# Second product of a split-word Winograd FFN: two matmuls for three, one of them 512 columns wide

## The chip, the core and the metric

The kernel runs on one NeuronCore of a Trainium2 chip. The metric is device time in microseconds (us). The kernel before takes 871.11 us, the median of three runs (870.78, 871.11 and 873.4). A profile of one execution shows its span, from the first to the last instruction, as 867.2 us. In this document PE is TensorE, PEld its weight loads, ACT is ScalarE, DVE is VectorE, POOL is GpSimd and SP is SyncE, which issues most DMAs.

## The reference

A linear attention with a normalisation feeds a feed-forward layer:

```python
kv  = einsum('bhsd,bhse->bhde', k, v)          # 8 batches, 8 heads, 576 tokens, 64 dims
o   = einsum('bhsd,bhde->bhse', q, kv)
x   = o / sqrt(mean(o*o) + 1e-6) * g_norm      # -> x: 4608 tokens x 512
h   = x @ w_in                                  # 512 -> 2048
g   = h * tanh(softplus(h))                     # Mish
out = g @ w_out                                 # 2048 -> 512, float32
```

The change touches the last line alone: `g @ w_out`, called the second product here.

## The kernel before

**Words.** Matrix operands are kept as two fp32r words each, a high one (the value rounded to fp32r) and a low one (what is left). A product of two such operands is made of three fp32r matmuls: low times high, high times low, high times high. `split` (L121) makes the words: ACT casts to the high word (L122), DVE subtracts to get the low word (L123).

**Blocks.** Each of the two big products is cut into 2 x 2 blocks and done with seven block products in place of eight (Winograd's form). The list `PROD` names them: A11*B11, S1*T1, A22*T4, S2*T2, A12*B21, S4*B22, S3*T3. The S forms are sums and differences of blocks of the left matrix, the T forms of the right one. The function `group` (L494) holds the order: its steps p0 to p6 each run one block product and register its take-out with `then`, for the next slot. A slot (L486) first writes the take-outs that are due, then the product, then other planned work. Step p2 belongs to the group before (its last product, A22*T4).

**The second product.** The 4608 tokens are cut into 18 groups of 256 (two halves of 128). A block product has 128 tokens, 1024 of the 2048 features (8 chunks of 128), and 256 of the 512 output columns. `mm_out` (L786) runs it: for each of the 8 chunks c three matmuls, with the words of g as stationary operand (128 x 128, loaded for each matmul) and a word of `w_out`'s form as moving operand of 256 columns; all 24 add into 256 columns of one PSUM bank (L790). The first group is done otherwise, with its own code at L904 to L911 (L908 in the profile); `mm_out` serves the other 17 groups, so 17 x 7 x 8 = 952 triples.

**Banks and take-outs.** There are two buffers named `a` and two named `bc`, each a tile of a whole bank (512 fp32 columns). Before, the second product uses the first 256 columns of each. Bank `a` collects p0, then p3, then p6 of its group, then p2 of the next slot round; bank `c` (a buffer of `bc`) collects p1 and then p5; bank `b` (the other) has p4. What stands in a bank after each step is taken out before the next step adds to it:

- p0, p1, p3 (L499, L504, L513) and the "21" block after p2 (L829) are copied to the output tile `ur` by ACT.
- After p4, p5, p6 (L835), DVE adds the bank to `ur`.

**Forms of g.** `g_load` brings 256 tokens of g from DRAM through SP, `g_form` (L763) makes one form: for S1 two DVE operations (L767, L768), for S2 and S4 one (L770, L772), and then the split. `ahead` (L924) keeps the forms three products ahead of the PE; it writes a form's instructions behind the product of each slot. ACT, DVE and PE run their instructions in the order in which they are written here.

**End.** After the last group's p6, the last A22*T4 is run alone, taken out by ACT (L829) and stored by DMA (L824).

Of the kernel before, what the change touches and what calls it, by code (L numbers as in the profile page):

```python
# [8 lines left out]
F32 = mybir.dt.float32  # L9
# [18 lines left out]
def linear_attention_rms_mish_ffn(  # L28
# [34 lines left out]
    nc = tc.nc  # L63
# [4 lines left out]
    P = 128  # L68
    R = 32
    T = 512  # L70
    TH = T // 2
# [3 lines left out]
    NF2 = NFC // 2  # L75
# [3 lines left out]
    NG = NTOK // G  # L79
# [10 lines left out]
    ps_m = ctx.enter_context(tc.tile_pool(name="ps_m", bufs=2, space=PSUM))  # L90
# [389 lines left out]
    def at(t, f):  # L480
        plan.setdefault(t, []).append(f)

    def then(t, f):
        evict.setdefault(t, []).append(f)

    def slot(t, product=None):  # L486
        for f in evict.pop(t, ()):
            f()
        if product:
            product()  # L490
        for f in plan.pop(t, ()):
            f()

    def group(st, t, mm, dst, put, prev):  # L494

        def p0():
            st["a"] = st["bank"]("a")
            mm(st, st["a"], A11, B11, True)
            then(t + 1, lambda: nc.scalar.copy(dst(st, "11"), st["a"]))  # L499

        def p1():
            st["c"] = st["bank"]("bc")
            mm(st, st["c"], S1, T1, True)
            then(t + 2, lambda: nc.scalar.copy(dst(st, "22"), st["c"]))  # L504

        def p2():
            if prev is not None:
                mm(prev, prev["a"], A22, T4, False)
                then(t + 3, lambda: put(prev, "21", prev["a"], t + 3))

        def p3():
            mm(st, st["a"], S2, T2, False)
            then(t + 4, lambda: nc.scalar.copy(dst(st, "12"), st["a"]))  # L513

        def p4():
            st["b"] = st["bank"]("bc")
            mm(st, st["b"], A12, B21, True)
            then(t + 5, lambda: put(st, "11", st["b"], t + 5))

        def p5():  # L520
            mm(st, st["c"], S4, B22, False)
            then(t + 6, lambda: put(st, "12", st["c"], t + 6))

        def p6():
            mm(st, st["a"], S3, T3, False)
            then(t + 7, lambda: put(st, "22", st["a"], t + 7))

        return p0, p1, p2, p3, p4, p5, p6

    def mm_in(st, bank, left, right, first):  # L530
# [65 lines left out]
    first, second = slice(0, 2), slice(2, NKC)  # L596
    nc.scalar.preload_act_table_set("natural_log_exp_and_others")
    weights(0, LOAD)
    t = wfp.tile([P, 3, 2 * T], F32, name="wf2")
# [67 lines left out]
    for b in range(2, B):  # L667
        t = NS * (b - 2)
# [26 lines left out]
    for j in range(1, NT):  # L695
        attention(j)
        if j == 1:
            for j in range(3, NF2):
                t = 3 * (j - 3) + 1
# [18 lines left out]


    wo = [None] * NF2  # L720
    gs = [{"s": s, "f": {}, "bank": lambda name: ps_m.tile([P, 2, TH], F32, name=name)[:, 0]} for s in range(NG)]
    rooms_made = 0

    def part2():
# [61 lines left out]
    def mm_out(st, bank, left, right, first):  # L786
        gf = st["f"][left]
        for c in range(NF2):
            for s, (a, b) in enumerate(((1, 0), (0, 1), (0, 0))):
                nc.tensor.matmul(  # L790
                    bank, gf[:, a, c, :], wo[c][:, :, right, b, :],
                    start=first and c == s == 0, stop=(c == NF2 - 1 and s == 2), skip_group_check=True,
                )

    def o_dst(st, block):
        if "o" not in st:
            st["o"] = up.tile([P, 2, DM], F32, name="ur")
        r, c = int(block[0]) - 1, int(block[1]) - 1
        return st["o"][:, r, c * G:(c + 1) * G]

    def o_store(st, of=range(2), cols=slice(0, DM), engines=(nc.sync,)):


        i, half = divmod(st["s"], T // G)
        w = cols.stop - cols.start
        if i < T32:
            for r in range(G // P):
                c = half * G // P + r
                for b, s0, seg in segments(i):
                    t0, t1 = max(seg.start, c * P), min(seg.stop, (c + 1) * P)  # L810
                    if t0 < t1:
                        row = b * S + s0 + t0 - seg.start
                        nc.sync.dma_start(out[row:row + t1 - t0, :], st["o"][t0 - c * P:t1 - c * P, r, :])
            return
        for m, n in enumerate((0, 2, 1, 3)):
            c = (half * G + n * R) // R
            for b, s0, seg in segments(i):
                first, L = seg.start // R, (seg.stop - seg.start) // R
                rs = [r for r in of if first <= c + r * P // R < first + L]
                if rs:  # L820
                    row = b * S + s0 + c + rs[0] * P // R - first
                    dst = out[row:row + 1, cols]
                    dst = bass.AP(dst.tensor, dst.offset, [[L * DM, R], [P // R * DM, len(rs)], [1, w]])
                    engines[m % len(engines)].dma_start(dst, st["o"][n * R:(n + 1) * R, rs[0]:rs[-1] + 1, cols])  # L824

    def put_out(st, block, bank, t):
        o = o_dst(st, block)
        if block == "21":
            nc.scalar.copy(o, bank)  # L829
            if st["s"] < NG - 1:  # L830
                at(t + 1, lambda: o_store(st))
            else:
                o_store(st, (1,), slice(0, G), (nc.sync, nc.scalar))
        else:
            nc.vector.tensor_add(o, bank, o)  # L835
            if st["s"] == NG - 1 and block == "12":
                o_store(st, (0,))
            if st["s"] == NG - 1 and block == "22":
                o_store(st, (1,), slice(G, DM))
# [28 lines left out]
    prev = None  # L868
    for i in range(NT):
        for n in range(NQ):  # L870
            st = {"i": i, "n": n, "bank": bank_new}
            t = NS * i + 7 * n
            for p, f in enumerate(group(st, t, mm_in, u_dst, put_in, prev)):
                slot(t + p, f)
            prev = st
    t = NS * NT
# [12 lines left out]
    bank = {w[0]: banks[b][:, h] for w, (b, h) in where.items()}  # L889
    st = gs[0]  # L890
    for n in range(NF2 // 2):
# [8 lines left out]
        for c in range(2):  # L900
# [3 lines left out]
            for (left, right), (b, h) in where.items():  # L904
                gf = st["f"][left, n]
                for s, (a, d) in enumerate(((1, 0), (0, 1), (0, 0))):
# [3 lines left out]
                        start=n == c == s == h == 0, stop=last_one, skip_group_check=True,  # L910
# [40 lines left out]
    for s in range(1, NG):  # L951
        for p, ((_, _, b), f) in enumerate(zip(PROD, group(gs[s], t, mm_out, o_dst, put_out, prev))):
            if b == "p" and prev is None:
                slot(t + p)
                continue
            used += 1
            slot(t + p, f)
            ahead(used + AHEAD)
        prev = gs[s]
        t += 7  # L960
    slot(t)
    mm_out(prev, prev["a"], A22, T4, False)
    slot(t + 1)
    put_out(prev, "21", prev["a"], t + 1)
    assert not plan and not evict, (sorted(plan), sorted(evict))

# [29 lines left out]
```

## Time and profile before

| what | value |
|---|---|
| time, median of 3 runs | 871.11 us (870.78 to 873.4) |
| span of the profiled execution | 867.2 us |
| PE busy over the span | 829.2 us, 96% |
| DVE busy, ACT busy | 604.5 us (70%), 462.4 us (53%) |
| one group of the second product, 684.50 to 704.70 us | PE busy 20.20 of 20.20 us, DVE 14.33, ACT 8.43, granted clock 1.00 |
| matmuls of L790, bank `a` and bank `bc` | 1632 and 1224 |

The profile gives no time of its own for the profiled execution beyond the span. The median of the runs is 3.9 us above the span. The page lists busy time by engine, the chain of work that ended last, and groups of equal instructions with their mean duration. A PE matmul's duration in it overlaps those of its neighbours, so the pace of matmuls is read from their starts, not from the durations. The view in order of time (a timeline) gives start, duration, engine, line, operation and, in brackets, the idle time of the engine before the instruction and what ended it.

### The profile page before, as it was taken

To read this page: it belongs to the slowest core of one execution; us is meant where nothing else is said; L and a number is where in the kernel's file an instruction comes from. 1 tells how busy PE (TensorE), PEld (TensorE's weight loads), DVE (VectorE), ACT (ScalarE), POOL (GpSimd) and SP (SyncE) were. 2 spreads that over 40 slices of the span, in tenths; PEclk is the share of its full clock that TensorE was granted. 3 is DMA by queue.
4 is the path that set the end of the run, shared out by engine and by line. 5 is a ranking of instruction groups with operands and counts; after the bars stand their busy time and mean duration, and the time that the engine had idled before them with its cause. 6 is when DMAs were issued, how large, how long until landed. Compare 5 with 4: busy or idle time off the path is not lost.

```text
span 867.2 us, 17267 instructions
## 1 busy us (share of the span) xinstructions
PE 829.2 (96%) x7036; PEld 799.0 (92%) x7036; DVE 604.5 (70%) x778; ACT 462.4 (53%) x681; POOL 102.5 (12%) x173
## 2 busy tenths in 40 slices
PE   4868999999999999999999999999999999999997
PEld 3656999999999999999899999999999999999997
DVE  4788676757766576677765788767767777776772
ACT  3666656655566656566666654444443344334441
POOL 2000122232222313112122100000000000000000
PEclk9889999999999999999999999999999999999999
DMA  9975686878877674757376972543444444344421
GB/s 277 258 230 150 202 261 229 282 240 276 249 234 224 217 228 168 239 182 271 128 233 239 383 260 78 179 145 114 134 131 122 122 122 122 122 125 147 148 69 49
DMA packets 121007, 164.52 MB, mean 190 GB/s; under 512 B 25184, under 2 KB 96096, under 8 KB 120672
## 3 DMA queue, kind: packets, MB, share of 16 engines
q1 hardware_dynamic: 107328, 116.42, 44.5%
q0 software_dynamic: 13504, 46.93, 14.4%
q8 instruction: 55, 0.90, 0.5%
q14 instruction: 24, 0.20, 0.1%
q10 hardware_dynamic: 96, 0.07, 0.0%
HBM read 106.89 MB, written 56.49 MB: 188 GB/s over the span
## 4 chain that ended last, share of the span: by engine, by line
PE 76%; ACT 9%; DVE 8%; issue 3%; DMA 2%; SPq 2%; ACTq 0%; DVEq 0%
PE a L790 22%; PE a L536 18%; PE bc L790 16%; PE bc L536 14%; PE s L261 2%; DVE gf L123 1%; ACT wf L122 1%; ACT gf L122 1%; SPq L304 1%; PE x L373 1%; ACT L421 1%; PE x L374 1%; DVE ur L557 1%; PE x L372 1%; DVE wf L123 1%
## 5 line engine op out<-in xcount | busy, mean ns | idle before, releaser
L790 PE MATMUL a<-wf,gf 128*128 128x256 f32 x1632 | 201.8, 283 | 0.5 <-DVE ur L835 0.5
L790 PEld LDWEIGHTS a<-wf,gf 128*128 128x128 f32 x1632 | 198.4, 192 | 0.7 <-DVE ur L835 0.7
L123 DVE TENSOR_TENSOR gf<-g,gf 128x1024 fp32r<-128x1024 f32 (+1 forms) x123 | 132.9, 1087 | 87.1 <-ACT gf L122 87.1
L536 PE MATMUL a<-gf,wf 128*128 128x256 f32 x1296 | 172.5, 286 | 6.9 <-ACT ur L513 6.6
L536 PE MATMUL bc<-gf,wf 128*128 128x256 f32 x1296 | 172.5, 286 | 2.1 <-ACT gf L122 1.9
L536 PEld LDWEIGHTS a<-gf,wf 128*128 128x128 f32 x1296 | 162.7, 192 | 12.3 <-ACT ur L513 8.3
L536 PEld LDWEIGHTS bc<-gf,wf 128*128 128x128 f32 x1296 | 163.3, 193 | 3.7 <-ACT gf L122 2.0
L122 ACT CAST gf<-g 128x1024 fp32r<-128x1024 f32 (+1 forms) x123 | 114.6, 939 | 90.7 <-DVE g L770 65.7
L790 PE MATMUL bc<-wf,gf 128*128 128x256 f32 x1224 | 152.7, 283 | 0.9 <-DVE gf L123 0.9
L790 PEld LDWEIGHTS bc<-wf,gf 128*128 128x128 f32 x1224 | 149.4, 192 | 1.3 <-ACT gf L122 0.7
L119 ACT ACTIVATE ur<-ur 128x1024 f32<-128x1024 f32 x36 | 38.1, 1059 | 54.7 <-DVE ur L557 54.7
L536 PE MATMUL a<-a,wf 128*128 128x256 f32 x432 | 58.8, 286 | 5.2 <-DVE ur L557 5.2
L536 PEld LDWEIGHTS a<-a,wf 128*128 128x128 f32 x432 | 55.1, 192 | 8.2 <-DVE ur L557 6.6
L123 DVE TENSOR_TENSOR fa<-fl,fh 128x1024 fp32r<-128x1024 f32 x28 | 34.2, 1221 | 18.1 <-ACT fh L122 16.9
L122 ACT CAST gf<-a 128x1024 fp32r<-128x1024 f32 x17 | 17.9, 1051 | 53.4 <-DVE a L767 50.9
L123 DVE TENSOR_TENSOR gf<-gf 128x512 fp32r<-128x512 f32 x45 | 30.2, 690 | 23.1 <-ACT gf L122 23.1
L513 ACT COPY ur<-a 128x512 f32<-128x512 f32 (+1 forms) x53 | 27.4, 517 | 32.2 <-PE a L790 24.6
L560 POOL DMA_DIRECT2D gd<-ula x36 | 26.1, 725 | 146.3 <-ACT ula L119 104.6
L122 ACT CAST gf<-gf 128x512 fp32r<-128x512 f32 x45 | 26.9, 618 | 30.1 <-DVE gf L460 17.5
L557 DVE TENSOR_TENSOR ula<-bc,ula 128x512 f32<-128x512 f32 x36 | 24.7, 686 | 23.8 <-PE bc L536 23.6
L504 ACT COPY ur<-bc 128x512 f32<-128x512 f32 (+1 forms) x53 | 27.5, 518 | 24.5 <-PE bc L790 23.0
L555 POOL DMA_DIRECT2D gd<-ulb x36 | 25.6, 711 | 94.7 <-ACT ulb L119 87.7
(147 smaller groups left out, 944.8 us busy)
## 6 DMA issues: line engine op xcount, KB each, us to landing
g<-gd SPq DMA_DIRECT2D x18, 2048.0 KB, 8.6
gd<-ur POOLq DMA_DIRECT2D x36, 512.0 KB, 5.1
gd<-ula POOLq DMA_DIRECT2D x36, 256.0 KB, 4.4
gd<-ulb POOLq DMA_DIRECT2D x36, 256.0 KB, 4.8
w<-in_moe_w_out_dram SPq DMA_DIRECT2D x32, 256.0 KB, 5.3
km<-in_k_dram SPq DMA_DIRECT2D x28, 256.0 KB, 4.4
vm<-in_v_dram SPq DMA_DIRECT2D x28, 256.0 KB, 4.9
wf<-wod SPq DMA_DIRECT2D x6, 896.0 KB, 8.0
```

The source lines that it names most:

```text
L119: nc.scalar.activation(o, i, AF.Mish)
L122: nc.scalar.copy(hi, src)
L123: nc.vector.tensor_sub(lo, src, hi.bitcast(F32))
L261: nc.tensor.matmul(kvps[o * D:(o + 1) * D, b % 2, h0 // 2 + i, :], kt, vt, start=(c == 0), stop=(c == CM))
L304: nc.sync.dma_start(rows[j][t0 - c * P:t1 - c * P, c, h0 * D:(h0 + n) * D].rearrange("p (h d) -> p h d", d=D), src)
L504: then(t + 2, lambda: nc.scalar.copy(dst(st, "22"), st["c"]))
L513: then(t + 4, lambda: nc.scalar.copy(dst(st, "12"), st["a"]))
L536: nc.tensor.matmul(bank[:, jj], w[:, right, a, kc, :], xf[:, b, kc, :], start=first and jj == kc == s == 0, stop=(kc == 1 and s == 2), ski ...
L555: at(t + 2, lambda: eng.dma_start(left[:, :, TH:T], o))
L557: nc.vector.tensor_add(o, bank, o)
L560: at(t + 3, lambda: eng.dma_start(left[:, :, 0:TH], o))
L790: nc.tensor.matmul(bank, gf[:, a, c, :], wo[c][:, :, right, b, :], start=first and c == s == 0, stop=(c == NF2 - 1 and s == 2), skip_group ...
```

## The change

Each triple of `mm_out` becomes two matmuls. The first has the high word of g as stationary operand and both words of `w_out`'s form side by side as moving operand, 512 columns: its result fills both halves of the bank, high times high in the first and high times low in the second. The second matmul has the low word of g and the high word of `w_out`, 256 columns, and adds to the first half. So the two halves of a bank have to be added when they are taken out: where ACT copied, ACT copies the first half and DVE adds the second (`take_out`); where DVE added 256 columns, it adds twice. The first product (`mm_in`) keeps its code, and gets its ACT copy under the name `take`. The first group of the second product (L904 to L911) is not changed.

```diff
-            then(t + 1, lambda: nc.scalar.copy(dst(st, "11"), st["a"]))
+            then(t + 1, lambda: st["take"](dst(st, "11"), st["a"]))
...
-            then(t + 2, lambda: nc.scalar.copy(dst(st, "22"), st["c"]))
+            then(t + 2, lambda: st["take"](dst(st, "22"), st["c"]))
...
-            then(t + 4, lambda: nc.scalar.copy(dst(st, "12"), st["a"]))
+            then(t + 4, lambda: st["take"](dst(st, "12"), st["a"]))
...
-    gs = [{"s": s, "f": {}, "bank": lambda name: ps_m.tile([P, 2, TH], F32, name=name)[:, 0]} for s in range(NG)]
+
+    def take_out(o, bank):
+        nc.scalar.copy(o, bank[:, 0])
+        nc.vector.tensor_add(o, bank[:, 1], o)
+
+    gs = [{"s": s, "f": {}, "bank": bank_new, "take": take_out} for s in range(NG)]
...
         for c in range(NF2):
-            for s, (a, b) in enumerate(((1, 0), (0, 1), (0, 0))):
-                nc.tensor.matmul(
-                    bank, gf[:, a, c, :], wo[c][:, :, right, b, :],
-                    start=first and c == s == 0, stop=(c == NF2 - 1 and s == 2), skip_group_check=True,
-                )
+            nc.tensor.matmul(
+                bank.rearrange("p s (h n) -> p s h n", h=2), gf[:, 0, c, :],
+                wo[c][:, :, right].rearrange("p h s n -> p s h n"),
+                start=first and c == 0, stop=False, skip_group_check=True,
+            )
+            nc.tensor.matmul(bank[:, 0], gf[:, 1, c, :], wo[c][:, :, right, 0, :], start=False, stop=c == NF2 - 1, skip_group_check=True)
...
         if block == "21":
-            nc.scalar.copy(o, bank)
+            take_out(o, bank)
...
-            nc.vector.tensor_add(o, bank, o)
+            for n in range(2):
+                nc.vector.tensor_add(o, bank[:, n], o)
...
-            st = {"i": i, "n": n, "bank": bank_new}
+            st = {"i": i, "n": n, "bank": bank_new, "take": nc.scalar.copy}
```

## The prediction

> **What bounds the kernel now.** I read the page first, then the time-ordered chain of waits, then busy time by stretch.
>
> ```profile
> span 867.2 us, 17267 instructions
> ...
> PE a L790 22%; PE a L536 18%; PE bc L790 16%; PE bc L536 14%; PE s L261 2%; DVE gf L123 1%; ACT wf L122 1%; ACT gf L122 1%; SPq L304 1%; PE x L373 1%; ACT L421 1%; PE x L374 1%; DVE ur L557 1%; PE x L372 1%; DVE wf L123 1%
> ...
> L790 PE MATMUL a<-wf,gf 128*128 128x256 f32 x1632 | 201.8, 283 | 0.5 <-DVE ur L835 0.5
> ...
> L790 PE MATMUL bc<-wf,gf 128*128 128x256 f32 x1224 | 152.7, 283 | 0.9 <-DVE gf L123 0.9
> ```
>
> L790, the line that changes, has 38% of the chain that ended last, and PE stood idle before it for 1.4 us in all. So this stage is bound by the pace of its matmuls.
>
> ```profile
> 680.81 2.88 PE bc L790 x24
> 683.69 5.76 PE a L790 x48
> ...
> 700.97 2.88 PE bc L790 x24
> ```
>
> In the chain, 24 matmuls take 2.88 us: one each 0.120 us. A group of seven block products takes 700.97 - 680.81 = 20.16 us.
>
> ```profile
> core 0: us, PE busy (x) PEld busy (x) DVE busy (x) ACT busy (x) POOL busy (x), PEclk, DMA share, GB/s
> 684.50:704.70 20.20, 20.20 (x171) 20.20 (x170) 14.33 (x15) 8.43 (x11) 0.00 (x0) 1.00 0.44 132
> ```
>
> The granted clock is full (1.00) there, so no gain can come from it. DVE is busy 14.33 of 20.20 us, and it is the engine that the change loads.
>
> **The matmuls: three starts become two.** The 256-column matmul that stays keeps 0.120 us. The new 512-column one with a 128 x 128 weight load has a counterpart in the first part, where the keys' product meets q (L372 to L374), in two runs of six:
>
> ```profile
> 406.58 0.40 PE L372 MATMUL x<-fh,kv 128*128 128x512 f32 x1
> ...
> 407.74 0.39 PE L374 MATMUL x<-fh,kv 128*128 128x512 f32 x1
> 407.97 0.52 PE L536 MATMUL bc<-gf,wf 128*128 128x256 f32 x3
> ...
> 424.76 0.39 PE L372 MATMUL x<-fh,kv 128*128 128x512 f32 x1
> ...
> 425.91 0.39 PE L374 MATMUL x<-fh,kv 128*128 128x512 f32 x1
> 426.13 0.64 PE L536 MATMUL bc<-gf,wf 128*128 128x256 f32 x4
> ```
>
> From the first start to the start of what follows: 407.97 - 406.58 = 1.39 us and 426.13 - 424.76 = 1.37 us, 2.76 us for twelve, so 0.230 us each. The last one of each run took 0.23 and 0.22. Two of 256 columns take 0.240, so the wide one saves about 10 ns. In the change wide and narrow ones take turns, which no row shows; I take 0.230, with the bounds 0.226 (below the shortest) and 0.236 (a little above the longest). The triple goes from 0.360 to 0.350 us, and 952 triples save 952 x 0.010 = 9.5 us (bounds: 13.3 and 3.8 us). A group would take 56 x 0.350 = 19.60 us.
>
> **The take-outs in the steady groups.** ACT copies as often as before. DVE gets seven more 128x256 additions per group: one behind each of four copies, one more at each of three additions. Their prices, and those of the queue they stand in:
>
> ```profile
> 683.51 1.23 DVE L772 TENSOR_TENSOR g<-g 128x1024 f32<-128x1024 f32 x1
> 685.90 1.23 DVE L123 TENSOR_TENSOR gf<-g,gf 128x1024 fp32r<-128x1024 f32 x1 [1.17 <-ACT gf L122]
> ...
> 692.37 0.42 DVE L835 TENSOR_TENSOR ur<-bc,ur 128x256 f32<-128x256 f32 x1 [0.30 <-PE bc L790]
> 692.71 1.21 DVE L767 TENSOR_TENSOR a<-g 128x1024 f32<-128x1024 f32 x1
> 693.96 1.22 DVE L768 TENSOR_TENSOR g<-g 128x1024 f32<-128x1024 f32 x1
> ```
>
> An addition takes 0.42 us. What follows it without touching its data starts 0.08 us before its end (692.71 against 692.79); what does touch it starts some 0.03 us after the end (693.96 against 693.92). So an addition costs DVE 0.34 us, or 0.45 us where it is the second into the same output. DVE's turn per group, if it never had to wait for PE: eleven operations of 1.225 us (seven splits, four sums of forms) make 13.5 us, ten additions of 0.42 us make 4.2; about 14 overlaps take off 1.2, five gaps add 0.2; and before the splits of S2 and S4 it waits for ACT's cast, 2 x 1.17 us (L123 above). The sum is 19.0 us, 0.6 us short of PE's 19.6. So DVE now runs nearly full, but PE should stay the bound. I walked the queue instruction by instruction with these durations, DVE, ACT and PE each in written order. A take-out then ends 0.9 to 2.7 us after its product, where before it was 0.4 to 1.5. The tightest reuse is bank `a`, two products after the step that filled it, 5.6 us: 2.9 us are left. The forms are ready 3 us or more before their product. So the additions cost nothing there: PE's own products cover them. Without that cover they would cost 7 x 0.34 = 2.4 us a group, 40 us over 17. The walk of the kernel before gives the two waits below and the end within 0.3 us.
>
> **The start, where the cover is missing.** The first group that `mm_out` serves has no p2 of a group before, so p3 follows p1 at once, and DVE is still late from the group written out by hand:
>
> ```profile
> 522.78 0.38 ACT L499 COPY ur<-a 128x256 f32<-128x256 f32 x1
> ...
> 525.81 1.22 DVE L123 TENSOR_TENSOR gf<-g,gf 128x1024 fp32r<-128x1024 f32 x1
> 527.06 1.23 DVE L772 TENSOR_TENSOR g<-g 128x1024 f32<-128x1024 f32 x1
> ...
> 517.97 3.04 PE L790 MATMUL a<-wf,gf 128*128 128x256 f32 x24
> ...
> 523.73 3.04 PE L790 MATMUL a<-wf,gf 128*128 128x256 f32 x24
> 527.17 3.11 PE L790 MATMUL bc<-wf,gf 128*128 128x256 f32 x24 [0.41 <-DVE gf L123]
> 530.83 0.95 PE L790 MATMUL bc<-wf,gf 128*128 128x256 f32 x6 [0.54 <-DVE gf L123]
> ```
>
> Now p3 waits for ACT's copy of p0 alone, which is long done (523.16), and starts at 523.73. After the change it waits for DVE's addition behind that copy, and that stands in DVE's queue behind the split of A12 (525.81 to 527.03): it ends at 527.03 + 0.34 = 527.37. PE took 0.14 us from DVE's end to its start (527.03 to 527.17), so p3 starts at 527.51, in place of 517.97 + 2 x 2.80 = 523.57: a wait of 3.9 us. Behind p3 on PE stands everything. But it swallows two waits that are there now: p4's, 527.17 - (523.73 + 2.88) = 0.56 us, and p5's, 530.83 - (527.17 + 2.88) = 0.78 us. p5 would start at 527.51 + 5.60 = 533.1, and its form (S4) is split by then even with the addition ahead of it: 527.37 + 1.23 (L772) + 1.17 (the wait for ACT's cast) + 1.23 (the split) = 531.0. So 3.9 - 1.3 = 2.6 us are lost, once. Bounds: 2.3 us if DVE's queue runs a little sooner; 3.5 us if the additions behind it delay p6 too.
>
> **The end.** The last product waits for the take-out of the last p6, and its own take-out ends the kernel:
>
> ```profile
> 859.40 0.42 DVE L835 TENSOR_TENSOR ur<-a,ur 128x256 f32<-128x256 f32 x1 [2.45 <-PE a L790]
> 859.88 3.13 PE L790 MATMUL a<-wf,gf 128*128 128x256 f32 x24 [0.52 <-DVE ur L835]
> ```
>
> That is the one stretch in which an addition lies open: a second addition ahead of the last product (0.45 us) and one behind the last copy (0.45 us), 0.9 us together. The stores behind them move with them.
>
> **The sum** against the span: -9.5 + 2.6 + 0.9 = -6.0 us, 867.2 to 861.2. Loading, part one and the first group are untouched, and the median of the runs is 3.9 us above the span, so I move it by the same: 871.1 - 6.0 = 865.1 us. With the bounds of the wide matmul alone it is 861.3 to 870.8.
>
> **Rivals.**
>
> (1) *Columns set the pace, and a start costs nothing*: slower. The short forms speak for it:
>
> ```profile
> 109.22 0.22 PE L372 MATMUL x<-fh,kv 128*128 128x128 f32 x1
> 109.28 0.28 PE L373 MATMUL x<-fa,kv 128*128 128x128 f32 x1
> ```
>
> 128 columns took 0.06 us, 256 take 0.120. By that 512 take 0.240, nothing is saved, and the waits at the start and the end stay: 871.1 + 3.5 = 874.6 us. It decides from 0.240 - 3.5/952 = 0.2363 us for the wide matmul on. Against it stand the twelve, 0.230 in the mean. [...]
>
> (2) *DVE becomes the bound*: slower. Its turn of 19.0 us rests on additions that overlap their neighbours. If the added waits on ACT's copies undo that for the independent pairs (no overlap: 14 x 0.08 = 1.2 us), the turn is 20.2 us, 0.6 over PE's; some of the lead of three forms is used up first, and 17 groups lose 17 x 0.6 = 10 us less about 1.5: 865.1 + 8.5 = 873.6 us. From a turn of 19.6 us it costs, from 19.6 + 6.0/17 = 19.95 us it makes the kernel slower. Against it: the additions of L835 wait for PE's semaphore too, and are overlapped.
>
> (3) *The wide matmul does better when the narrow one follows it*, 0.226 us or less, the last of the second run pointing there (426.13 - 425.91 = 0.22): 13.3 us saved, 861.3 us.
>
> (4) *A middle*: the wide one takes 0.234 us, or DVE costs a few waits: 5.7 - 3.5 = 2.2 us saved, 868.9 us.
>
> **How the numbers follow.** The forecast (862 to 868) 0.58; rival 1 0.11, rival 2 0.12, rival 3 0.07, rival 4 0.12. A measurement of this kernel tells 0.3% (2.6 us) from no change. Faster: 0.58 + 0.07 and a little of rival 4, 0.66. Same: the rest of rival 4 and the light cases of 1 and 2, 0.17. Slower: 0.17. The range 861 to 873.5 leaves about 0.06 below and 0.13 above. The likeliest case's own range is 862 to 868.
>
> **What would show it.** Starts in the steady groups: 2.80 us a block product and 19.6 us a group. If a group takes 20.16 us without waits on PE, rival 1 holds. If PE waits on DVE in every group, rival 2. DVE should be busy 16.5 to 17.5 us a group. At the start PE should wait some 3.9 us for DVE's take-out ahead of p3, and the waits ahead of p4 and p5 should be gone. The end should be 0.9 us longer behind the last steady product. I am wrong if p3 doesn't wait, if waits show in the steady groups, or if the triple isn't near 0.350 us.

## The result and the profile after

The changed kernel takes 864.86 us, the median of 15 runs (860.79 to 871.34), against 871.11 us for the kernel before (15 runs, 868.65 to 873.4). The ratio is 0.9942, with a 95% interval of 0.9921 to 0.9962: 0.6% faster. The predicted time was 865.1 us. The mechanism came out as forecast; that the number came out so near is partly luck, as terms of its sum were off in opposite directions and the times of the changed kernel fall into two clusters, above and below it.

The profiled execution of the changed kernel is one of the quicker ones, 861.15 us. From its page (L794 is the wide matmul, L799 the narrow one):

```profile
span 859.4 us, 15464 instructions
...
PE 816.9 (95%) x6084; PEld 746.0 (87%) x6084; DVE 643.3 (75%) x897; ACT 459.5 (53%) x681; POOL 102.8 (12%) x173
...
L794 PE MATMUL a<-wf,gf 128*128 128x512 f32 x544 | 191.8, 394 | 4.8 <-DVE ur L724 3.7
...
L794 PE MATMUL bc<-wf,gf 128*128 128x512 f32 x408 | 143.1, 391 | 0.0
```

The same line of the page before:

```profile
PE 829.2 (96%) x7036; PEld 799.0 (92%) x7036; DVE 604.5 (70%) x778; ACT 462.4 (53%) x681; POOL 102.5 (12%) x173
```

There are 952 fewer matmuls (6084 for 7036), each with its weight load, and 119 more DVE instructions (897 for 778). PE waits 3.7 us ahead of L794 for L724, the added addition, and 1.1 us ahead of the last product; there is no other wait of note in this stage.

The timeline of PE in a steady group (start, duration, engine, line):

```profile
640.09 0.39 PE L794 MATMUL bc<-wf,gf 128*128 128x512 f32 x1
640.32 0.28 PE L799 MATMUL bc<-wf,gf 128*128 128x256 f32 x1
640.43 0.39 PE L794 MATMUL bc<-wf,gf 128*128 128x512 f32 x1
...
641.12 0.39 PE L794 MATMUL bc<-wf,gf 128*128 128x512 f32 x1
```

A triple is still called so, though it is two matmuls now. Three triples take 641.12 - 640.09 = 1.03 us. In the trace's nanoseconds the starts lie 230 and 117 or 116 apart: 346.7 ns per triple, 56 x 0.3467 = 19.41 us per group. Before it was 360 ns and 20.16 us.

The busy time by stretch of a steady group, with the columns of the prediction's table:

```profile
562.60:582.00 19.40, 19.40 (x113) 17.10 (x113) 16.55 (x21) 8.22 (x12) 0.00 (x0) 1.00 0.40 134
```

PE is busy all the time, and DVE is busy 16.55 us of 19.40, where it was 14.33 of 20.20. The additions are there, and no PE time is lost to them.

The start, in the timelines of PE and DVE and in the stretches:

```profile
517.61 0.40 PE L794 MATMUL a<-wf,gf 128*128 128x512 f32 x1
...
523.15 0.28 PE L799 MATMUL bc<-wf,gf 128*128 128x256 f32 x1
527.13 0.49 PE L794 MATMUL a<-wf,gf 128*128 128x512 f32 x1 [3.71 <-DVE ur L724]
...
531.48 0.49 PE L794 MATMUL bc<-wf,gf 128*128 128x512 f32 x1
```

```profile
525.53 1.22 DVE L123 TENSOR_TENSOR gf<-g,gf 128x1024 fp32r<-128x1024 f32 x1
526.66 0.42 DVE L724 TENSOR_TENSOR ur<-a,ur 128x256 f32<-128x256 f32 x1
```

```profile
526.90:528.30 1.40, 1.17 (x7) 1.04 (x8) 1.31 (x2) 0.00 (x0) 0.00 (x0) 0.99 0.46 176
528.30:531.70 3.40, 3.40 (x13) 2.92 (x12) 2.32 (x3) 2.26 (x3) 0.00 (x0) 0.50 0.00 0
```

p3 waits as forecast, for the addition of p0 that stands behind the split of A12. But the wait has a second price: from 528.3 to 531.7 the granted clock is 0.50. p3's eight triples take 531.48 - 527.13 = 4.35 us in place of 2.77. The waits ahead of p4 and p5 are gone, as forecast.

The end, in the timelines of PE, ACT and DVE:

```profile
850.39 0.28 PE L799 MATMUL a<-wf,gf 128*128 128x256 f32 x1
851.74 0.47 PE L794 MATMUL a<-wf,gf 128*128 128x512 f32 x1 [1.07 <-DVE ur L842]
```

```profile
854.79 0.37 ACT L723 COPY ur<-a 128x256 f32<-128x256 f32 x1 [11.08 <-PE a L799]
855.65 0.86 ACTq L830 DMA_DIRECT2D out_dram<-ur  x2
```

The end of the kernel before:

```profile
863.05 0.37 ACT L829 COPY ur<-a 128x256 f32<-128x256 f32 x1 [10.96 <-PE a L790]
863.45 0.86 ACTq L824 DMA_DIRECT2D out_dram<-ur  x2
```

From the last copy's start to the store it is now 0.86 us (before 0.40), and the last product starts 1.35 us behind the matmul before it (before 0.80).

### The profile page after: what moved, and what is told of

Read it like the earlier page. It is cut to its first block, busy times and chain, and to the rows that moved or that the text cites. A ratio compares the mean times of both kernels' runs of the same rounds, so it can differ in the third digit from the quotient of the medians.

```text
span 859.4 us, 15464 instructions
## 1 busy us (share of the span) xinstructions
PE 816.9 (95%) x6084; PEld 746.0 (87%) x6084; DVE 643.3 (75%) x897; ACT 459.5 (53%) x681; POOL 102.8 (12%) x173
## 4 chain that ended last, share of the span: by engine, by line
PE 75%; ACT 9%; DVE 9%; issue 3%; SPq 2%; DMA 2%; ACTq 0%; DVEq 0%
PE a L536 18%; PE a L794 14%; PE bc L536 13%; PE bc L794 11%; PE a L799 7%; PE bc L799 6%; PE s L261 2%; DVE gf L123 1%; ACT wf L122 1%; ACT gf L122 1%; SPq L304 1%; DMA vm<-in_v_dram 1%; DVE fl L150 1%; DVE fl L149 1%; ACT L119 1%
## 5 line engine op out<-in xcount | busy, mean ns | idle before, releaser
L794 PE MATMUL a<-wf,gf 128*128 128x512 f32 x544 | 191.8, 394 | 4.8 <-DVE ur L724 3.7
L799 PE MATMUL a<-wf,gf 128*128 128x256 f32 x544 | 153.0, 281 | 0.0
L794 PE MATMUL bc<-wf,gf 128*128 128x512 f32 x408 | 143.1, 391 | 0.0
L794 PEld LDWEIGHTS a<-wf,gf 128*128 128x128 f32 x544 | 102.4, 188 | 27.8 <-DVE ur L724 4.0
L799 PE MATMUL bc<-wf,gf 128*128 128x256 f32 x408 | 114.2, 280 | 0.0
L799 PEld LDWEIGHTS a<-wf,gf 128*128 128x128 f32 x544 | 103.5, 190 | 0.0
L794 PEld LDWEIGHTS bc<-wf,gf 128*128 128x128 f32 x408 | 76.4, 187 | 16.8
L799 PEld LDWEIGHTS bc<-wf,gf 128*128 128x128 f32 x408 | 77.2, 189 | 0.0
```

What stands on the lines that cost most here:

```text
L794: nc.tensor.matmul(bank.rearrange("p s (h n) -> p s h n", h=2), gf[:, 0, c, :], wo[c][:, :, right].rearrange("p h s n -> p s h n"), start= ...
L799: nc.tensor.matmul(bank[:, 0], gf[:, 1, c, :], wo[c][:, :, right, 0, :], start=False, stop=c == NF2 - 1, skip_group_check=True)
```

## The experiments

**The change again, twice.** No edit. Of the first 15 runs of the change, eight lay at 860.8 to 864.9 us and seven at 868.7 to 871.3, with none between.

> The changed kernel once more, unaltered. Theory (fewer matmul starts, additions hidden in the steady groups, one wait at the start and one at the end): a group of seven block products again takes 19.4 us without a wait of PE, the wait ahead of p3 of the first group is 3.7 to 4 us, and the median lies 5 to 9 us under the kernel before. The runs of the changed kernel so far fall into two clusters, 861 to 865 and 869 to 871 us. If the clusters come from the change, they show here again and not in the kernel before; if they come from the chip of that day, both kernels scatter alike here.

Measured: 863.71 us, the median of 12 runs (861.64 to 869.75), ratio 0.9944 (0.9921 to 0.9966). Seven runs lie at 861.6 to 864.0, one at 866.7, four at 868.3 to 869.8; the kernel before lies at 868.4 to 873.3 in 17 runs. So the changed kernel scatters over 8 us, the kernel before over 5 us. The profiled execution was that of 866.71 us. It has 19.41 us per group too; its second group starts at 522.34 us, 4.7 us later than in the first trace of the change. That much of the scatter comes from the first part of the kernel, which the change doesn't touch, and it is about the scatter of the kernel before. Another 0.8 us come from the clock, which stays at 0.50 for 6.8 us in this trace. The 10 us of the change need a second cause.

> The changed kernel once more, for its trace. The traces so far show the triple at one of two paces that hold for whole stretches: 346.7 ns (wide 230, narrow 117) or 353.4 ns (starts 351, 361 and 349 apart, in turns). Theory (the pace makes the two clusters of times): 952 triples at 6.7 ns more are 6.4 us; a run near 862 us has 19.41 us per group, one near 869 us has 19.79 us per group, whatever the first part of the kernel does. Rival (the clusters come from the first part): 19.41 us per group in both, and the start of the second group 6 us later in the slow one.

Measured: 870.21 us, one run, of the upper cluster. The timeline of PE, in a steady group:

```profile
639.76 0.40 PE L794 MATMUL a<-wf,gf 128*128 128x512 f32 x1
640.00 0.28 PE L799 MATMUL a<-wf,gf 128*128 128x256 f32 x1
640.11 0.40 PE L794 MATMUL a<-wf,gf 128*128 128x512 f32 x1
640.35 0.28 PE L799 MATMUL a<-wf,gf 128*128 128x256 f32 x1
640.46 0.40 PE L794 MATMUL a<-wf,gf 128*128 128x512 f32 x1
...
640.82 0.40 PE L794 MATMUL a<-wf,gf 128*128 128x512 f32 x1
```

and the stretch:

```profile
603.90:623.70 19.80, 19.80 (x113) 17.18 (x113) 16.55 (x23) 8.22 (x11) 0.00 (x0) 1.00 0.43 133
```

The same program, the same granted clock of 1.00, no wait of PE, and yet three triples take 640.82 - 639.76 = 1.06 us in place of 1.03. In the trace's nanoseconds the wide matmuls start 349, 350 and 361 apart, in turns: 353.3 ns per triple and 19.79 us per group, in all steady groups. A wide one takes 236.5 ns in the mean (232 to 241) and a narrow one 117, so it is the wide one that is slower. 952 triples at 6.7 ns are 6.3 us, and the clusters lie 6 to 7 us apart. The theory holds as far as three traces of the change can show it: two have the faster pace in their steady groups and one the slower. The pace is a mean: in the trace of 866.71 us its 346.7 ns are made of 344 and 350 in turns.

**The take-outs alone.** The three narrow matmuls of before, one of them into the second half:

```diff
-            nc.tensor.matmul(
-                bank.rearrange("p s (h n) -> p s h n", h=2), gf[:, 0, c, :],
...
-            nc.tensor.matmul(bank[:, 0], gf[:, 1, c, :], wo[c][:, :, right, 0, :], start=False, stop=c == NF2 - 1, skip_group_check=True)
+            for s, (a, b) in enumerate(((0, 1), (0, 0), (1, 0))):
+                nc.tensor.matmul(
+                    bank[:, b], gf[:, a, c, :], wo[c][:, :, right, b, :],
+                    start=first and c == s == 0, stop=(c == NF2 - 1 and s == 2), skip_group_check=True,
+                )
```

> The take-outs alone: three matmuls of 256 columns per triple as before, the one with the low words of the right matrix into the second half of the bank, and the two halves added as in the change. Theory: the triple is back at 0.360 us and a group at 20.16 us, nothing is saved, and the wait at the start (3.9 us in place of 1.3, and about 1.4 us more at a halved clock behind it) and at the end (0.9 us) stay: 4 to 5 us slower than before, 875 to 876 us. Rival (the gain comes from how the bank or the words are used and not from the number of matmuls): faster than before.

Measured: 876.18 us, ratio 1.0066 (1.0046 to 1.0086), all six runs at 874.8 to 877.5.

```profile
640.00:660.20 20.20, 20.20 (x171) 20.20 (x170) 16.68 (x22) 8.22 (x11) 0.00 (x0) 1.00 0.43 132
```

A group takes 20.16 us without waits, as before, with DVE busy for 16.68 us. So the gain belongs to the two matmuls in place of three. Each matmul brings its own weight load (7036 of each on the page of before, 6084 of each on that of the change), so the runs don't tell the price of a matmul's start from that of a load. The take-outs cost 5.8 us in the traces, counted from the second product's first matmul to the end: 4.8 in the first group and 1.0 at the end. That is a little more than expected, as the clock is 0.51 in the mean from 529 to 535 us here. There is one cluster: without the wide matmul the second pace didn't show in six runs.

**The matmuls alone.** The second half of the bank isn't added:

```diff
     def take_out(o, bank):
         nc.scalar.copy(o, bank[:, 0])
-        nc.vector.tensor_add(o, bank[:, 1], o)
...
-            for n in range(2):
-                nc.vector.tensor_add(o, bank[:, n], o)
+            nc.vector.tensor_add(o, bank[:, 0], o)
```

> The matmuls alone: two matmuls per triple as in the change, but the second half of the bank is never added, so the products of g's high words with the low words of the right matrix are left out of the result; the take-outs are those of before. Theory: a group takes the same 19.4 us as in the change, because the additions are hidden there, and the waits at the start and the end are those of before: 12.4 us faster than before, 858 to 860 us. Rival (the additions cost something in every group, DVE's queue as the bound): a group shorter than in the change by more than 0.1 us, and the gain over the change more than 6 us.

Measured: 858.47 us, ratio 0.9874 (0.9842 to 0.9906); five runs at 856.8 to 859.6, one at 865.1.

```profile
640.00:659.40 19.40, 19.40 (x115) 17.10 (x114) 14.29 (x15) 8.44 (x11) 0.00 (x0) 1.00 0.44 134
```

The group takes the same 19.4 us with 14.29 us of DVE as with 16.55: in the steady groups the additions are free. From the second product's first matmul to the end it takes 336.8 us, against 341.8 in the first trace of the change; of these 5.0 us, 4.1 lie in the first group and 0.9 at the end.

**DVE loaded further.** Seven small additions per group into a spare tile, from the third group on:

```diff
             slot(t + p, f)
+            for _ in range(1 if s > 1 else 0):
+                nc.vector.tensor_add(spare, ident, ident)
```

> The change with one more DVE addition of 128x128 in each slot from the third group on, seven per group, into a spare tile (some 0.21 us each where it overlaps its neighbour, 1.5 us per group). Theory (DVE's own turn is 19.0 us): with 20.5 us it becomes the bound, a group takes 20.3 to 20.6 us, PE waits for take-outs and forms in every group, and the kernel is some 15 us slower than the change. Rival (DVE has more room than worked out, since its waits for ACT's casts shrink when it is late): a group stays at 19.4 to 19.8 us without waits of PE.

Measured: 875.16 us, one run. The waits of PE in the second product and a stretch:

```profile
PEld a L794 <- DVE ur L724: 13.6, 14, 4.0
PE a L794 <- DVE ur L724: 9.2, 13, 3.7
```

```profile
640.00:660.30 20.30, 20.07 (x115) 17.32 (x114) 17.80 (x29) 8.04 (x11) 0.00 (x0) 1.00 0.42 130
```

After three groups at 19.41 us, in which the lead of the forms is used up, the groups take 20.0 to 20.5 us, 20.25 in the mean of twelve. PE waits 13 times for L724, once at the start and 12 times in these groups. Almost no wait of DVE for PE is left, so this is DVE's own turn with seven additions of 0.20 us (1.4 us) more in it. Without them it is some 18.9 us: the 19.0 us worked out were right within 0.2, and the change has about half a microsecond per group to spare. From the second product's first matmul to the end it is 11.8 us slower than the first trace of the change, not 15, because the first groups live on the lead and the later ones lose 0.6 to 1.1 us each.

**The wait at the start.** The sums of the first group's output are written four slots later:

```diff
-    nc.scalar.copy(o12, bank[A11])
...
-    o_store(st)
+    def first_out(st=st, bank=bank):
+        nc.scalar.copy(o12, bank[A11])
...
+        o_store(st)
...
     t += 8
+    at(t + 4, first_out)
```

> The change with the sums of the first group's output (one copy and seven additions, about 3.1 us of DVE) written four slots later, behind p4 of the second group, so that they don't stand ahead of the take-out of p0. Theory (p3 waits for DVE's queue): the wait ahead of p3 falls from 3.9 us to about 1 us, the clock isn't halved behind it, and the kernel is 3 to 5 us faster than the change, 859 to 862 us; DVE carries the 3 us of lateness into the next groups, whose slack of 2.9 us nearly covers it. Rival (the wait is only moved): the 3 us come back as waits in the following two groups, and the time is that of the change.

Measured: 864.81 us, ratio 0.9927 (0.99 to 0.9955): one run at 859.16, five at 864.1 to 866.8. The timeline of PE, and a stretch:

```profile
524.45 0.28 PE L799 MATMUL bc<-wf,gf 128*128 128x256 f32 x1
525.46 0.51 PE L794 MATMUL a<-wf,gf 128*128 128x512 f32 x1 [0.73 <-DVE ur L724]
525.81 0.28 PE L799 MATMUL a<-wf,gf 128*128 128x256 f32 x1
525.92 0.39 PE L794 MATMUL a<-wf,gf 128*128 128x512 f32 x1
```

```profile
640.00:659.80 19.80, 19.80 (x114) 17.16 (x113) 16.54 (x21) 8.27 (x12) 0.00 (x0) 1.00 0.44 134
```

The starts lie 1.0 us apart where they lay 4.0 apart, and the two matmuls behind the first one take 0.28 and 0.39 us, as at a clock of 1.00: so far as these show it, the theory holds there. But the time missed, and hardly by the rival: the second group loses 0.4 us to a wait, the later ones nothing, yet they take 19.8 us. This trace has the slower pace throughout. At the faster one it would be 6.3 us shorter, an estimate from the two paces; from the second product's first matmul to the end that is 337.5 us, against 341.8 in the first trace of the change, so the later sums are worth some 4 us. By their times five of the six runs have the slower pace, and 12 or so of the 28 runs of the change; six runs are too few to say that the edit makes it more likely.

**Where the pace comes from.** Three traces have this in common, two of the change and that of the later sums: the stream starts at the slower pace, straight out of the first group's matmuls (in the first trace of the change 236 ns in the mean for a wide one and 117 for a narrow one, from 517.61 to 523.15 us). In the first trace of the change (span 859.4 us) it changed to 346.7 ns behind the wait and the halved clock; in that with a span of 868.4 us it had the same wait and returned to 353.3; with the matmuls alone it is 346.7 ns in the steady groups, behind two waits of 0.7 us together. With DVE loaded further, twelve waits of 0.2 to 0.9 us stand in the later groups, and behind them the pace was the faster one eight times and the slower one four times. So a wait can change the pace and needn't. Two orders were tried. First the narrow one ahead of the wide one:

```diff
+            nc.tensor.matmul(bank[:, 0], gf[:, 1, c, :], wo[c][:, :, right, 0, :], start=first and c == 0, stop=False, skip_group_check=True)
             nc.tensor.matmul(
                 bank.rearrange("p s (h n) -> p s h n", h=2), gf[:, 0, c, :],
...
-                start=first and c == 0, stop=False, skip_group_check=True,
+                start=False, stop=c == NF2 - 1, skip_group_check=True,
             )
-            nc.tensor.matmul(bank[:, 0], gf[:, 1, c, :], wo[c][:, :, right, 0, :], start=False, stop=c == NF2 - 1, skip_group_check=True)
```

> The change with the 256-column matmul of each triple ahead of the 512-column one. Theory (two stable paces, and which one is taken hangs on how the stream of matmuls starts again after a wait): the paces are again 346.7 and 353.4 ns and no others, perhaps in other shares; median 861 to 870 us. Rival (the slower pace belongs to a wide matmul ahead of a narrow one at the start of each product): the slower pace is gone, and the times lie in one cluster at 861 to 864 us.

Measured: 866.68 us, ratio 0.9954 (0.9929 to 0.9978), five runs at 862.3 to 864.9 and five at 868.5 to 872.9. The timeline of PE in its trace (868.84 us):

```profile
639.95 0.40 PE L795 MATMUL a<-wf,gf 128*128 128x512 f32 x1
...
641.01 0.40 PE L795 MATMUL a<-wf,gf 128*128 128x512 f32 x1
```

Three triples take 1.06 us, the slower pace, and a group 19.79 us. Both clusters stay; the rival falls. Then two chunks together:

```diff
-        for c in range(NF2):
+        for c0 in range(0, NF2, 2):
+            for c in (c0, c0 + 1):
+                nc.tensor.matmul(
+                    bank.rearrange("p s (h n) -> p s h n", h=2), gf[:, 0, c, :],
...
+            for c in (c0, c0 + 1):
+                nc.tensor.matmul(bank[:, 0], gf[:, 1, c, :], wo[c][:, :, right, 0, :], start=False, stop=c == NF2 - 1, skip_group_check=True)
```

> The change with the matmuls of two chunks together: two of 512 columns, then two of 256. Theory (a fixed 13.3 ns for each start at best, whatever the order): 693 ns for the two triples, as in the faster pace, 19.41 us per group, 861 to 864 us. Rival (wide matmuls behind each other take the 230 ns and more that they take in the first part, where six stand in a row at 229 to 231 ns): 2 x 230 + 2 x 120 = 700 ns, 19.6 us per group, some 3 us slower than the faster pace.

Measured: 863.72 us, ratio 0.9928 (0.9909 to 0.9946), six runs in one cluster, 862.9 to 866.4. The timeline of PE:

```profile
639.77 0.62 PE L795 MATMUL a<-wf,gf 128*128 128x512 f32 x2
...
640.47 0.63 PE L795 MATMUL bc<-wf,gf 128*128 128x512 f32 x2
...
641.17 0.62 PE L795 MATMUL bc<-wf,gf 128*128 128x512 f32 x2
```

A group takes 19.51 us, 348.3 ns per triple: midway between the two expectations (346.7 and 350). In the six runs no second cluster showed, so this order looks like one with a single pace; six runs don't prove it.

**Both edits together,** the later sums and the pairs:

> Both edits together: the sums of the first group's output four slots later, and the matmuls of two chunks together (two wide, two narrow). Theory (the wait at the start and the pace add up, and this order has one pace only): 19.5 us per group in the trace as with the pairs alone, about 1 us of wait ahead of p3, times in one cluster at 858.5 to 861.5 us, some 3 us under the pairs alone. Rival (DVE's lateness of 3 us comes back as waits because its queue is nearly full): 862 to 864 us.

Measured: 861.29 us, five runs at 858.8 to 861.9, ratio 0.988 (0.9862 to 0.9898).

```profile
526.22 0.74 PE L795 MATMUL a<-wf,gf 128*128 128x512 f32 x2 [0.82 <-DVE ur L724]
```

```profile
640.00:659.50 19.50, 19.50 (x114) 17.01 (x113) 16.52 (x22) 8.23 (x13) 0.00 (x0) 1.00 0.44 136
```

From the second product's first matmul to the end the trace takes 339.5 us, against 343.3 with the pairs alone: the later sums gain 3.8 us here. The rival shows in part, as a wait that costs the second group 0.7 us. The kernel is 1.2% faster than before, twice the change's gain, and the best of the kernels that compute the whole result.

**Four chunks together,** with `range(0, NF2, 4)` and the later sums kept:

> The same with the matmuls of four chunks together (four wide, four narrow). Theory (two paces belong to a strict turn of wide and narrow; in longer rows a wide takes 0.230 to 0.233 us and a narrow 0.115 to 0.120, as in the first part): 347 to 352 ns per triple, one cluster, within 2 us of the pairs. Rival (rows of equal matmuls come nearer to the best pace the longer they are): 346.7 ns, 1.5 us faster than the pairs.

Measured: 863.80 us, six runs at 861.8 to 864.7, ratio 0.991 (0.9896 to 0.9925); 19.65 us per group, 350.8 ns per triple. One cluster again, but 2.5 us slower than the pairs with the later sums: a longer row of equal matmuls is no better than two, and the rival falls.

## Why the prediction was right, point by point

The first trace of the change against that of before, in its own spans (859.4 and 867.2, so -7.8 us):

| term | predicted | measured |
|---|---|---|
| 952 triples | -9.5 | -12.7 at the faster pace (-6.3 at the slower) |
| additions in the steady groups | 0 | 0 |
| wait ahead of p3, less the two waits that it swallows | +2.6 | +2.5 |
| half clock behind that wait (1.6), and the products until the faster pace is reached (0.2) | not seen | +1.8 |
| end, ahead of the last product and behind its copy | +0.9 | +1.0 |
| first part, scatter | 0 | -0.4 |
| sum | -6.0 | -7.8 |

- **The bound** was read rightly: the pace of the matmuls, with everything else beneath it. The take-outs alone gained nothing and cost 5.8 us; the matmuls alone gained more than the change.
- **The triple** is the term that was mis-sized. "I take 0.230, with the bounds 0.226 ... and 0.236" was said of a wide matmul in a row of its own kind. In turns with narrow ones the wide one takes 230 to 232 ns in the traces with the faster pace, close to what was assumed, and 236.5 in the slower, just beyond the upper bound. The narrow one, which was to keep 120 ns, takes 115 to 117 in both. The 0.350 of the forecast lies between the two sums, 346.7 and 353.3, and is neither. Against the 360 ns of before, one matmul fewer saves 13.3 ns at the faster pace and 6.7 at the slower.
- **The steady groups**: DVE's turn of 19.0 us held, and so did its busy time of 16.5 to 17.5 us a group. Its loading showed where the room ends, and leaving the additions out gained nothing there.
- **The start**: the wait was 527.13 - 523.15 - 0.12 = 3.9 us as forecast, for the reason that was given. What was missed is what a wait of that length does to the clock: it was 0.50 for 3.4 us in one trace of the change, which cost 1.6 us, and for 6.8 us in that of 866.71 us, where p3 takes 5.29 us in place of 2.77, a cost of 2.5. In the trace of 870.21 us p3 begins at the pace of the halved clock, its starts behind the wait 0.60 and 0.21 us apart, where the first trace has 0.34 and 0.11. Where two starts lay only 1.0 us apart, with the later sums, the next matmuls took 0.28 and 0.39 us, as at 1.00. In the trace of 866.71 us the clock falls at 530.30 us, 2.2 us after PE's last matmul ended and 1.5 us before the next.
- **The end** was right: 0.55 us ahead of the last product and 0.46 us behind its copy, for 0.45 and 0.45.
- **The rivals**: rival 1 (columns alone) and rival 2 (DVE as the bound) did not come. The rows that spoke for rival 1 were the first two of three: the next 128-column matmuls start 0.12 and 0.11 us apart, not 0.06. Rival 3's time of 861.3 us came in the faster runs, but there it is the narrow matmul that is shorter, not the wide one. Rival 4's 868.9 us came in the slower runs, with its triple of 0.354 us (353.3 ns measured), made of 236.5 and 117 rather than 234 and 120. The forecast of 865.1 us stands between the two clusters, where few single runs lie.

## What to carry to other kernels

Merging two matmuls with the same stationary operand saved 7 to 13 ns of 360 here; the columns stay the same, 768 a triple. It is worth it where PE sets the pace and the engine that must join the halves has room in its own turn. Add up that engine's turn with its waits, not its busy share, and look for the places where the cover is missing: the first group and the last. A wait of 4 us on PE cost more than itself here, 1.6 to 2.5 us, through the clock behind it. Moving work that nobody waits for out of the queue ahead of it was worth 3.8 us on top of the pairs.

## What the runs showed of the hardware that was not expected

A stream of matmuls of 512 and 256 columns in turns ran at one of two paces, 346.7 or 353.3 ns for the two, and kept it until the next wait, at the same granted clock of 1.00. A wait could move the stream from one to the other. The stream of 256 columns alone kept 120 ns a matmul, and two wide with two narrow ones took 348.3 ns per triple. What in PE or its weight loads makes the two paces was not found; the order of wide and narrow within a triple is not it.

In the trace of 866.71 us the clock fell 2.2 us after PE's last matmul ended. In the traces of before and of the first run of the change each stretch of one clock but the last is 3.41 us long or a whole multiple of it (6.83, 17.07, 27.31 us and more); a step here is one of 3.41 us. In the first trace of the change PE was busy for 2.00 us of the 3.42 ahead of 524.85 us, and the clock stayed at 1.00; it was busy for 1.13 us of the 3.41 ahead of 528.26 us, and the clock was 0.50 for the next step. In the trace of 866.71 us it was 1.25 us of the 3.40 ahead of 530.30 us, and then:

```profile
530.30:537.10 6.80, 5.29 (x17) 4.51 (x17) 5.28 (x6) 2.26 (x3) 0.00 (x0) 0.50 0.20 77
```

In the trace of before PE was busy for 1.67 us of the 3.41 ahead of 495.79 us, and the clock was 0.50 for the next step; but it was busy for 1.69 us of the 3.41 ahead of 89.60 us, and the clock stayed at 1.00. So PE's busy share of the step before doesn't decide it alone; what does stays open.
